# First q and k loads in halves of four heads, with one more unread matmul and a reordered column step, in an attention + MLP kernel

## The chip, the cores and the metric

The kernel runs on one core of a Trainium2 chip. The metric is the device time of one launch in microseconds (us). Before the change it is 356.62 us, the median of three runs (356.17 to 357.84).

The engines of the core work side by side, each through its own list of instructions in order: PE (TensorE, matrix products; its weight loads are listed as PEld), DVE (VectorE), ACT (ScalarE), POOL (GpSimd) and SP (SyncE). POOL, SP and ACT also issue DMA transfers, which all run on the same 16 DMA engines.

## What is computed

Attention with a forgetting gate over 8 batches of 8 heads, 576 positions and head size 64, and then a two-layer MLP on all 4608 rows:

```python
scores = scale * np.matmul(q, k.transpose(0, 1, 3, 2))
cum = np.cumsum(np.log(np.clip(f, 0.0001, 1.0)), axis=-1)
decay = cum[:, :, :, None] - cum[:, :, None, :]
scores = np.where(causal, -1000000000.0, scores + decay)   # causal: above the diagonal
attn = softmax(scores)
x = (attn @ v), heads side by side                # 4608 x 512
h = x @ w_in                                      # 512 -> 2048
out = (h - np.tanh(h)) @ w_out                    # 2048 -> 512
```

Inputs and output are float32; the kernel computes in float16 with float32 sums.

## The kernel before

**Batches.** Batch 0 has code of its own, written so that work begins as soon as the first rows are there; the others go by pairs of heads (`slot`, L481), and the MLP's steps (`step`, L455: `mlp1`, then `mlp2`, for 512 rows at a time) are dealt out among them by hand. The order on every engine is the order in which the code is written out (L497 to L601); there is no scheduler.

**Loading batch 0.** Each block of 128 positions of q and of k (the fifth has 64) is one DMA issued by POOL through `load_first` (L88): 128 positions by 8 heads by 64 values, converted from float32 to float16 on the way. The order on POOL is: q and k of block 0; a select that makes the identity matrix `id16` (L129), needed by every transpose; q and k of block 1; a select that makes the triangle `tri16` (L133), the mask of the diagonal; q and k of block 2; then, mixed with blocks 3 and 4, the five blocks of v (`load_v`), the first half of w_in (`load_win`, L523), q and k of batch 1 (`load_qk`), the second half of w_in, later v and q, k of batch 1, w_out (L575), and at last q and k of batch 2 whole (`LOADS`, L200), which is issued in `slot`. A DMA uses one of eight semaphores in turn, so an issue waits until the eighth DMA before it has landed.

**Using it.** `half0(ib, a, ...)` (L269) takes block `ib` and half `a` of the heads: `trans0` (L247) turns four heads of q and four of k with eight PE transposes (L254) into one PSUM tile, and two copies, one for q and one for k (`copy0`, L260, on DVE or ACT), bring them to `QT` and `KT`. `scores0` (L274) multiplies them (L282), adds the mask on the diagonal with a second matmul (L285, `neg16` times `tri16`), and takes the exponential on ACT (L287). `values0` (L289) multiplies with v (L295).

**The decay columns.** The running sum of log f goes into extra columns of q and k, so that the score's matmul adds it. `decay_turn` (L171) turns it on PE (L176), and `decay_cols(b0, b1)` (L178) writes the columns for blocks b0 to b1 with three DVE operations (L181, L183, L184). Blocks 0 and 1 get theirs before the first transposes; blocks 2 to 4 at L508.

**Unread matmuls.** `spin(n)` (L221) issues n matmuls of 128 by 512 on a constant, whose result nobody reads. Eight stand at the start (L497) and one before the first transposes (L503).

**Batch 1 and 2.** Their q and k come in whole rows and are turned by `trans` (L227, six transposes each, L236): those of batch 2's first pair of heads stand in the fourth slot of batch 1, between score and MLP matmuls.

Of the kernel before, what the change touches and what calls it, by code (L numbers as in the profile page):

```python
# [22 lines left out]
def kernel(  # L23
# [10 lines left out]
    nc = tc.nc  # L34
    P = 128

    B, H, S, D = q.shape
# [28 lines left out]
    ps_m = ctx.enter_context(tc.tile_pool(name="ps_m", bufs=3, space=PSUM))  # L66
# [4 lines left out]
    XR = wpl.tile([P, NCH, RING], FP16)  # L71

    HH = H // 2
    raw = [[qkp.tile([P, RW], FP16, tag=f"{x}n{i}", name=f"{x}n{i}") for i in range(2)] for x in "qk"]
    qn, kn = ([t[0:S // NT6, :].rearrange("p (h n d) -> p h n d", h=H, n=NT6) for t in ts] for ts in raw)
    qa, ka = (t[0][:, 0:NJ * H * AW].rearrange("p (n h d) -> p n h d", n=NJ, h=H) for t in raw)
# [8 lines left out]
        pn = min(P, S - n * P)  # L85
        nc.gpsimd.dma_start(out=dst[0:pn, n, h0:h1, 0:D], in_=src[b, h0:h1, n * P:n * P + pn, :].rearrange("h p d -> p h d"))  # L86

    def load_first(dst, src, n):  # L88
        p0 = max(0, (n + 1) * P - S)
        nc.gpsimd.dma_start(out=dst[p0:P, n, :, 0:D],  # L90
                            in_=src[0, :, n * P:(n + 1) * P - p0, :].rearrange("h p d -> p h d"))

    def turn_block(dst, src, b, n):
        pn = min(P, S - n * P)
# [5 lines left out]
    def load_v(b, n):  # L100
        load_block(vn[b % 2], v, b, n)
# [22 lines left out]
    nc.vector.memset(ones16, 1.0)  # L124
    nc.vector.memset(id16, 0.0)
    nc.vector.memset(tri16, 0.0)
    load_first(qa, q, 0)
    load_first(ka, k, 0)
    nc.gpsimd.affine_select(out=id16, in_=id16, compare_op=ALU.not_equal,  # L129
                            fill=1.0, base=0, pattern=[[-1, P]], channel_multiplier=1)  # L130
    load_first(qa, q, 1)
    load_first(ka, k, 1)
    nc.gpsimd.affine_select(out=tri16, in_=tri16, compare_op=ALU.is_ge,  # L133
                            fill=BIG, base=0, pattern=[[1, P]], channel_multiplier=-1)
    nc.vector.memset(vn[0][:, :, :, D:VW], 1.0)
# [35 lines left out]
    def decay_turn(blocks):  # L171
        if not CT:
            CT.append(ps_tr.tile([P, UW], FP32, tag="tr", name="ct"))
        for ib in blocks:
            t0 = min(ib * P, S - P)
            nc.tensor.transpose(out=CT[0][:, ib * H:(ib + 1) * H], in_=cum[0:H, t0:t0 + P], identity=id32)  # L176

    def decay_cols(b0, b1):  # L178
        ct = CT[0][:, b0 * H:b1 * H].rearrange("p (n h) -> p n h", h=H)
        hi = ka[:, b0:b1, :, D]  # L180
        nc.vector.tensor_scalar(out=qa[:, b0:b1, :, D + 2], in0=ct, scalar1=inv_qscale,  # L181
                                scalar2=-SHIFT * inv_qscale, op0=ALU.mult, op1=ALU.add)
        nc.vector.tensor_scalar_mul(out=hi, in0=ct, scalar1=inv_qscale)  # L183
        nc.vector.scalar_tensor_tensor(out=ka[:, b0:b1, :, D + 1], in0=ct, scalar=inv_qscale, in1=hi,  # L184
                                       op0=ALU.mult, op1=ALU.subtract)
# [16 lines left out]
    for b in range(2, B):  # L202
        p0 = (b - 1) * NPAIR
# [17 lines left out]
    def spin(n):  # L221
        av = ps_av.tile([P, 2, 512], FP32, tag="av", name="spin")
        for _ in range(n):
            nc.tensor.matmul(out=av[:, 0, :].rearrange("p (a n) -> p a n", n=P), lhsT=one128[:, 0, :],  # L224
                             rhs=one128.to_broadcast([P, UW // P, P]))
# [21 lines left out]
    def trans0(ib, a, pool, engs):  # L247
        p0 = max(0, (ib + 1) * P - S)
        pn = P - p0
        t32 = pool.tile([P, UW], FP32, tag="tr" if pool is ps_tr else "m", name="t32")  # L250
        t16 = t32.bitcast(FP16)[0:D + 3, 0:H * pn].rearrange("p (x h n) -> p x h n", x=2, h=HH)
        for x, src in enumerate((qa, ka)):
            for h in range(HH):
                nc.tensor.transpose(out=t16[:, x, h, :], in_=src[p0:P, ib, a * HH + h, 0:D + 3],  # L254
                                    identity=id16[p0:P, p0:P])
        T0[(ib, a)] = t16, engs
# [3 lines left out]
    def copy0(ib, a, x):  # L260
        w = min(P, S - ib * P)
        t16, engs = T0[(ib, a)]
        to = (QT, KT)[x][0][:, a * HH:(a + 1) * HH, ib * P:ib * P + w]
        if engs[x] == "A":
            nc.scalar.activation(out=to, in_=t16[:, x, :, :], func=AF.Copy)
        else:
            nc.vector.tensor_copy(out=to, in_=t16[:, x, :, :])

    def half0(ib, a, pool, engs):  # L269
        trans0(ib, a, pool, engs)  # L270
        copy0(ib, a, 0)
        copy0(ib, a, 1)

    def scores0(ib, ti):  # L274
        w = min(P, S - ib * P)
        n = UW // w
        ps = ps_sc.tile([P, 512], FP32, tag="sc", name="ps")
        e = aex.tile([P, 512], FP16, tag="e", name="e")
        todo = [(h, j) for h in range(H) for j in range(ib + 1)][n * ti:n * ti + n]
        for i, (h, j) in enumerate(todo):  # L280
            at = slice(i * w, (i + 1) * w)
            nc.tensor.matmul(out=ps[:, at], lhsT=KT[0][:, h, j * P:(j + 1) * P],  # L282
                             rhs=QT[0][:, h, ib * P:ib * P + w], start=True, stop=(j < ib))
            if j == ib:
                nc.tensor.matmul(out=ps[:, at], lhsT=neg16, rhs=tri16[:, 0:w], start=False, stop=True)  # L285
            E[(0, h, j, ib)] = e[:, at]
        nc.scalar.activation(out=e, in_=ps, func=AF.Exp, scale=qscale)  # L287

    def values0(ib):  # L289
        w = min(P, S - ib * P)  # L290
        av = ps_av.tile([P, 2, 512], FP32, tag="av", name="av")
        av = av[0:w, :, 0:HH * (D + 1)].rearrange("p i (h d) -> p i h d", h=HH)
        for h in range(H):
            for j in range(ib + 1):
                nc.tensor.matmul(out=av[:, h // HH, h % HH, :], lhsT=E.pop((0, h, j, ib)),  # L295
                                 rhs=vn[0][:, j, h, 0:D + 1], start=(j == 0), stop=(j == ib))
# [205 lines left out]
    nc.vector.tensor_scalar_mul(out=neg16, in0=id16, scalar1=-BIG)  # L502
    spin(1)  # L503
    half0(0, 0, ps_m, "VA")
    half0(0, 1, ps_m, "VV")
    scores0(0, 0)
    decay_turn((2, 3, 4))
    decay_cols(2, NJ)  # L508
    half0(1, 0, ps_m, "VV")
    scores0(0, 1)  # L510
    half0(1, 1, ps_m, "VV")
    load_first(qa, q, 2)
    load_first(ka, k, 2)
    load_v(0, 0)
    load_v(0, 1)
    load_first(qa, q, 3)
    load_first(ka, k, 3)
    load_v(0, 2)
    load_v(0, 3)
    load_first(qa, q, 4)  # L520
    load_first(ka, k, 4)
    load_v(0, 4)
    load_win(0, DFF // 2)  # L523
    for h in (0, 2):
# [105 lines left out]
```

## Time and profile before

| | |
|---|---|
| median of three runs | 356.62 us |
| the profiled execution | 356.36 us |
| its span, first to last instruction | 354.6 us |
| PE busy | 347.9 us (98%) |
| ACT busy | 222.9 us (63%) |
| DVE busy | 192.6 us (54%) |
| POOL busy | 150.3 us (42%) |
| moved by DMA | 38.70 MB in 148,583 packets |
| chain that ended last | PE 92%, DVE 4%, ACT 3% |

The profile is of one execution. A timeline row gives start and duration in us, the engine, the line, the operation, what it writes and reads, and how often; in brackets the engine's idle time before it and what ended it. `x2` means that two instructions are merged in the row. A matmul's duration runs to its end in the pipeline, so that neighbours overlap: what a row costs PE is the distance to the next start. Of a DMA issued by POOL the row's duration is POOL's work to issue it; the landing is given apart, counted from the issue's start. In rows of shares over 40 slices each digit is the busy share in tenths, 9 for 90% and more.

### The profile page before, as it was taken

Reading aid. Unit: us, or ns where it says so; the run is one execution under the profiler, and the core shown is the slowest. Engines: PE = TensorE matmul, PEld = TensorE weight load, DVE = VectorE, ACT = ScalarE, POOL = GpSimd, SP = SyncE. Lnnn points to the kernel's source line nnn. Section 1 sums busy time; section 2 is a strip of 40 time slices with the busy share of each in tenths; the row PEclk is TensorE's granted clock in tenths of the full one; section 3 lists DMA queues with packets and bytes.
Section 4 is the critical chain, followed back from the end, with each engine's and each line's share of the span. In section 5 each row is a group of like instructions: output and inputs, shape, how many; then the busy total and the mean of one; then the engine's idle time right before and its main releaser. Section 6 shows DMA issues by size and latency. Waiting matters only on the chain.

```text
span 354.6 us, 7878 instructions
## 1 busy us (share of the span) xinstructions
PE 347.9 (98%) x3002; PEld 203.1 (57%) x3002; DVE 192.6 (54%) x364; ACT 222.9 (63%) x411; POOL 150.3 (42%) x291
## 2 busy tenths in 40 slices
PE   7989999999999999999999999999999999999996
PEld 4978886555555555555558865555555554444443
DVE  6587887449851676167715681478137513812720
ACT  4587886357755885588557865786568734613620
POOL 8954523653477537662776277632222210000000
PEclk9999999999999999999999999999999999999999
DMA  9999999999299949998999979991220022011002
GB/s 91 143 202 187 205 183 153 158 179 151 28 108 173 149 87 114 146 151 114 76 152 183 115 59 140 167 142 31 88 74 16 8 74 76 2 53 66 2 30 89
DMA packets 148583, 38.70 MB, mean 109 GB/s; under 512 B 137346, under 2 KB 143042, under 8 KB 148546
## 3 DMA queue, kind: packets, MB, share of 16 engines
q0 software_dynamic: 100128, 18.36, 72.5%
q1 hardware_dynamic: 48338, 19.78, 29.0%
q8 instruction: 23, 0.38, 0.5%
q14 instruction: 14, 0.11, 0.2%
q10 hardware_dynamic: 80, 0.07, 0.1%
HBM read 36.85 MB, written 9.44 MB: 131 GB/s over the span
## 4 chain that ended last, share of the span: by engine, by line
PE 92%; DVE 4%; ACT 3%; issue 1%; ACTq 0%; DVEq 0%
PE ops L442 34%; PE hps L415 30%; PE ps L340 10%; PE av L368 7%; PE hps L401 3%; PE ps L282 1%; PE t L254 1%; ACT e L287 1%; DVE gt L391 1%; DVE KT L245 1%; PE spin L224 1%; PE ops L426 1%; PE t L236 1%; ACT th L389 1%; PE av L295 1%; PE ps L285 1%
## 5 line engine op out<-in xcount | busy, mean ns | idle before, releaser
L442 PE MATMUL ops<-wout,gt 128*128 128x512 f16 x560 | 136.8, 378 | 0.0
L391 DVE TENSOR_TENSOR gt<-hps,th 128x512 f16<-128x512 f32 x144 | 99.0, 690 | 58.9 <-ACT th L389 58.2
L349 ACT ACTIVATE e<-ps 128x512 f16<-128x512 f32 x168 | 99.3, 594 | 46.9 <-PE ps L340 40.1
L415 PE MATMUL hps<-XR,win 128*128 128x512 f16 (+1 forms) x576 | 125.6, 355 | 0.2
L389 ACT ACTIVATE th<-hps 128x512 f32<-128x512 f32 x144 | 86.0, 597 | 29.0 <-PE hps L415 22.9
L359 POOL TENSOR_SCALAR_AFFINE_SELECT e<-e 128x128 f16<-128x128 f16 x144 | 48.7, 338 | 102.7 <-ACT e L349 100.2
L442 PEld LDWEIGHTS <-gt 128*128 128x128 f16 x560 | 50.3, 97 | 51.0
L415 PEld LDWEIGHTS <-win 128*128 128x128 f16 x576 | 52.3, 97 | 44.3 <-issue 0.5
L340 PE MATMUL ps<-QT,KT 67*128 67x512 f16 (+1 forms) x336 | 70.7, 277 | 0.4 <-ACT e L349 0.2
L340 PEld LDWEIGHTS <-KT 67*128 67x128 f16 x336 | 32.8, 98 | 33.5 <-DVE KT L245 0.2
L446 ACT ACTIVATE ost<-ops 128x512 f32<-128x512 f32 x35 | 20.9, 597 | 36.4 <-PE ops L442 36.4
L374 DVE TENSOR_SCALAR rs<-av 128x10 f32<-128x10 f32 x28 | 4.6, 164 | 68.4 <-PE av L368 68.3
L86 POOL DMA_DIRECT2D vn<-in_v_dram x40 | 34.2, 862 | 11.4 <-DMA win<-in_moe_w_in_dram 3.6
L368 PEld LDWEIGHTS <-e 128*128 128x128 f16 x784 | 28.1, 97 | 5.5
L368 PE MATMUL av<-vn,e 128*128 128x65 f16 x784 | 29.1, 193 | 0.0
L86 POOL DMA_DIRECT2D qn<-in_q_dram x25 | 21.2, 848 | 11.3 <-PE t L236 6.1
L376 DVE TENSOR_TENSOR xn<-av,rs 128x640 f16<-128x640 f32 x28 | 23.1, 825 | 1.0
L86 POOL DMA_DIRECT2D kn<-in_k_dram x25 | 21.3, 852 | 1.4 <-issue 1.2
L287 ACT ACTIVATE e<-ps 128x512 f16<-128x512 f32 x25 | 14.4, 596 | 6.6 <-PE ps L285 4.6
L401 PE MATMUL hps<-XR,win 128*128 128x256 f16 x128 | 16.6, 272 | 0.0
L282 PE MATMUL ps<-QT,KT 67*128 67x128 f16 (+1 forms) x120 | 12.0, 220 | 1.5 <-ACT e L287 0.7
L245 DVE COPY QT<-t 64x576 f16<-64x576 f16 x12 | 9.6, 801 | 6.5 <-PE t L236 5.1
(83 smaller groups left out, 221.3 us busy)
## 6 DMA issues: line engine op xcount, KB each, us to landing
out_dram<-ost SPq DMA_DIRECT2D x35, 256.0 KB
vn<-in_v_dram POOLq DMA_DIRECT2D x32, 128.0 KB, 5.5
qn<-in_q_dram POOLq DMA_DIRECT2D x24, 128.0 KB, 3.8
kn<-in_k_dram POOLq DMA_DIRECT2D x24, 128.0 KB, 4.8
win<-in_moe_w_in_dram POOLq DMA_DIRECT2D x2, 1024.0 KB, 12.2
wout<-in_moe_w_out_dram POOLq DMA_DIRECT2D x4, 512.0 KB, 11.9
XR<-xn SPq DMA_TRANSPOSE x56
qn<-in_q_dram POOLq DMA_DIRECT2D x1, 576.0 KB, 17.6
```

What stands on the lines that cost most here:

```text
L86: nc.gpsimd.dma_start(out=dst[0:pn, n, h0:h1, 0:D], in_=src[b, h0:h1, n * P:n * P + pn, :].rearrange("h p d -> p h d"))
L340: nc.tensor.matmul(out=ps[:, col:col + n], lhsT=KT[b % 2][0:D + 3, h, j * P:(j + 1) * P], rhs=QT[b % 2][0:D + 3, h, i0:i0 + n], start=True ...
L349: nc.scalar.activation(out=e[:, lo:hi], in_=ps[:, lo:hi], func=AF.Exp, scale=qscale)
L359: nc.gpsimd.affine_select(out=view, in_=view, compare_op=ALU.is_ge, fill=0.0, base=0, pattern=pat, channel_multiplier=-1)
L368: nc.tensor.matmul(out=av[:, a, ib, :], lhsT=E.pop((b, 2 * c + a, j, ib)), rhs=vn[b % 2][:, j, 2 * c + a, 0:D + 1], start=(j == 0), stop=( ...
L376: nc.vector.tensor_tensor(out=xn.rearrange("p i (a d) -> p a i d", a=2), in0=av[:, :, :, 0:D], in1=rs.to_broadcast([P, 2, NJ, D]), op=ALU. ...
L389: nc.scalar.activation(out=th, in_=hps, func=AF.Tanh, scale=-1.0)
L391: nc.vector.tensor_tensor(out=gt, in0=hps, in1=th, op=ALU.add)
L401: nc.tensor.matmul(out=hps[:, w * SB:(w + 1) * SB], lhsT=win[:, ci, ft * P:(ft + 1) * P], rhs=XR[:, ci, t * SB:(t + 1) * SB], start=(ci == ...
L415: nc.tensor.matmul(out=hps[:, o:o + n], lhsT=win[:, ci, s * P:(s + 1) * P], rhs=XR[:, ci, t:t + n], start=(ci == 0), stop=(ci == NCH - 1))
L442: nc.tensor.matmul(out=ops, lhsT=GT[(u, ft, m)], rhs=wout[:, ft, :], start=(ft == 0), stop=(ft == NFT - 1))
L446: nc.scalar.activation(out=ost, in_=ops, func=AF.Copy)
```

## The change

q and k of blocks 0, 1 and 2 of batch 0 are loaded in two DMAs of four heads each, where they were one of eight; blocks 3 and 4 stay whole. On POOL, the identity's select comes after the first half of block 0, and the triangle's select after both halves of block 1. One more unread matmul stands between the two halves of block 0 on PE. The columns of blocks 2 to 4 are written after the copies of block 1's first half instead of before them; the turn on PE that feeds them stays where it was.

```diff
+    HALVES = ((0, HH), (HH, H))
...
-    def load_first(dst, src, n):
+    def load_first(n, heads=((0, H),)):
         p0 = max(0, (n + 1) * P - S)
-        nc.gpsimd.dma_start(out=dst[p0:P, n, :, 0:D],
-                            in_=src[0, :, n * P:(n + 1) * P - p0, :].rearrange("h p d -> p h d"))
+        for h0, h1 in heads:
+            for dst, src in ((qa, q), (ka, k)):
+                nc.gpsimd.dma_start(out=dst[p0:P, n, h0:h1, 0:D],
+                                    in_=src[0, h0:h1, n * P:(n + 1) * P - p0, :].rearrange("h p d -> p h d"))
...
-    load_first(qa, q, 0)
-    load_first(ka, k, 0)
+    load_first(0, HALVES[0:1])
     nc.gpsimd.affine_select(out=id16, in_=id16, compare_op=ALU.not_equal,
                             fill=1.0, base=0, pattern=[[-1, P]], channel_multiplier=1)
-    load_first(qa, q, 1)
-    load_first(ka, k, 1)
+    load_first(0, HALVES[1:2])
+    load_first(1, HALVES)
     nc.gpsimd.affine_select(out=tri16, in_=tri16, compare_op=ALU.is_ge,
                             fill=BIG, base=0, pattern=[[1, P]], channel_multiplier=-1)
...
     half0(0, 0, ps_m, "VA")
+    spin(1)
     half0(0, 1, ps_m, "VV")
     scores0(0, 0)
     decay_turn((2, 3, 4))
+    half0(1, 0, ps_m, "VV")
     decay_cols(2, NJ)
-    half0(1, 0, ps_m, "VV")
     scores0(0, 1)
     half0(1, 1, ps_m, "VV")
-    load_first(qa, q, 2)
-    load_first(ka, k, 2)
+    load_first(2, HALVES)
     load_v(0, 0)
     load_v(0, 1)
-    load_first(qa, q, 3)
-    load_first(ka, k, 3)
+    load_first(3)
     load_v(0, 2)
     load_v(0, 3)
-    load_first(qa, q, 4)
-    load_first(ka, k, 4)
+    load_first(4)
```

## The prediction

> **What bounds the kernel now.** I read the page first (PE busy 98% of the 354.6 us span, the chain 92% PE), then the waits after 30 us (one wait over 0.15 us on PE), so nearly all idle time of PE lies in the first 30 us, the stage that the change touches. There I read PE's timeline.
>
> ```profile
> 6.62 0.61 PE L254 MATMUL t<-id,kn 128*67 128x128 f16 x4 [0.56 <-DVE neg L502]
> 8.37 0.29 PE L282 MATMUL ps<-QT,KT 67*128 67x128 f16 x1 [0.29 <-ACT KT L265]
> 10.61 0.31 PE L282 MATMUL ps<-QT,KT 67*128 67x128 f16 x1
> 10.71 0.31 PE L285 MATMUL ps<-tri,neg 128*128 128x128 f16 x1
> 13.98 0.22 PE L285 MATMUL ps<-tri,neg 128*128 128x128 f16 x1
> 14.04 0.28 PE L282 MATMUL ps<-QT,KT 67*128 67x128 f16 x2
> ```
>
> Each starts with start and duration in us. PE has two holes, before 6.62 and before 8.37. Matmuls of 128 columns start 0.11 us apart at 10.6 and 0.06 apart at 14: the clock doubles at about 13.2. (The granted clock is given as 1.00 in every window; the spacing says otherwise.)
>
> Then POOL, which issues every load of q, k, v and the weights, in order.
>
> ```profile
> 1.33 1.01 POOL L90 DMA_DIRECT2D qn<-in_q_dram  x1 [0.82 <-POOLq L614]
> ...
> 5.63 0.89 POOL L90 DMA_DIRECT2D qn<-in_q_dram  x1
> 6.51 0.88 POOL L90 DMA_DIRECT2D kn<-in_k_dram  x1
> 7.38 1.77 POOL L86 DMA_DIRECT2D vn<-in_v_dram  x2
> ...
> 13.24 0.77 POOL L90 DMA_DIRECT2D kn<-in_k_dram  x1
> 13.91 0.77 POOL L86 DMA_DIRECT2D vn<-in_v_dram  x1
> 14.58 0.86 POOL L188 DMA_DIRECT2D win<-in_moe_w_in_dram  x1
> 15.33 0.75 POOL L196 DMA_DIRECT2D qn<-in_q_dram  x1
> ```
>
> From 1.33 to 20 POOL does nothing but issue, two short selects aside. A whole block of 128 rows and 8 heads takes 0.87 us from start to start (5.63, 6.51, 7.38); the fifth block, 64 rows and half as many pieces, takes 0.67 (13.24, 13.91, 14.58). Half the pieces save a quarter.
>
> Last I asked where these loads come due. The whole of batch 2's q and k is issued at 37.23 and 38.01; the views of these two issues, q then k:
>
> ```profile
> who waited for it (us, times):
>   PEld L236: 0.2, 1
> ...
> DMA to landing us min/median/max: 17.6/17.6/17.6
> ```
> ```profile
> DMA to landing us min/median/max: 19.8/19.8/19.8
> ```
> ```profile
> 54.76 0.22 PE L343 MATMUL ps<-tri,neg 128*128 128x128 f16 x1
> 54.89 0.43 PE L236 MATMUL t<-id,qn 96*128 96x96 f16 x6
> ...
> 57.64 0.19 PE L343 MATMUL ps<-tri,neg 128*128 128x64 f16 x1
> 57.81 0.43 PE L236 MATMUL t<-id,kn 96*128 96x96 f16 x6
> ```
> ```profile
> DMA  9999999999999999999999999999999999999999
> ```
>
> 37.23 + 17.6 = 54.8 and 38.01 + 19.8 = 57.8: PE's transposes of them (L236) start at 54.89 and 57.81, the moment they land, with gaps of 0.13 and 0.17 us where the same mask matmul is followed 0.06 and 0.03 later elsewhere. So PE and the loads arrive together: the loads have no slack. The last row is the DMA engines' share in 40 slices of 16 to 58 us: never under 90%. From 16 us on this is one unbroken stream; whatever starts it later lands those two later.
>
> **The change, part by part.**
>
> *Halves on POOL.* Six loads become twelve. A half is [128 rows, 4 heads], 512 pieces; no row shows it. Bounds: half of a whole one, 0.44 (shift 0), and as much as a whole one, 0.87 (shift 5.2 us). The nearest rows are the fifth block (512 pieces, 0.67) and the 128x4 shape of wout, 0.74 us each when issued alone, win 0.75 (14.58 to 15.33). I take 0.72: 12 x 0.72 - 6 x 0.87 = 8.6 - 5.2 = 3.4 us. POOL's issues also wait for the eighth one before them to land (4.15 us idle before wout's at 32.66, ended by win's landing); eight halves take 5.8 us to issue and about 3.1 to land, so that wait isn't met. SP's queue has nothing moved. Everything behind it on POOL moves by the 3.4: v0 from 7.38 to 10.8, block 3's k from 9.97 to 13.4, the first weights from 14.58 to 18.0. With 0.67 it is 2.8. The triangle's select, which stood behind four loads (5.38), now stands behind eight: 1.33 + 0.86 + 0.74, the identity's select 0.4, then 6 x 0.72 end at 7.7, so the triangle is there at 8.0; its reader, the first mask matmul, ran at 8.45.
>
> The Trainium skill's page "DMA: Bandwidth & Descriptors" speaks on both sides. Its section on the anatomy of a software-issued DMA puts dispatch at some 50 ns and calls descriptor generation small, so by it six more issues are an estimated 0.3 us and the sum stays at 356.4. The rows above have 0.7 to 0.9 us of POOL for each issue and decide against that. Its rules for kernel authors say of two halves that they share the same engines and aren't worth splitting, which is the sum taken here.
>
> *The stream behind it.* Part of the 3.4 us is given back, because the DMA engines were somewhat behind in the first 17 us: block 3's k landed 4.5 us after its issue and the fifth v block, a half-size one, 4.3, where the first q had taken 3.6. A half-size load without a backlog is 3.6 - 0.2 (shorter issue) - 0.43 (half of the 0.87 between landings) = 3.0, so the backlog at the weights was 1.3 to 1.4 us. With slower issue it doesn't build. 3.4 - 1.4 = 2.0 us later for win and all that follows. Bounds: 0.8 (issue at 0.62, the smallest issue's spacing, 15.33 to 15.96: shift 2.2, less 1.4) and 3.4 (no backlog given back).
>
> *Who meets it.* win: 14.58 + 9.8 = 24.4, plus 2.0 is 26.4; first reader L401 at 27.34: hidden, 0.9 to spare. Batch 1's loads have 2.6 us and more (its last q 27.12 + 10.9 = 38.1 for 40.72): hidden; with 3.4 late it would cost 0.8. Batch 2's q and k have none: PE waits 2.0 us at 54.89. Behind that wait stands all of PE's order, and PE is 98% busy from there to the end, so it is paid in full.
>
> *The start.* The first halves land earlier: k's is issued at 2.2 and lands about 3.2 later, 5.4, where the whole landed at 2.34 + 4.1 = 6.5. Its transposes can follow q's at 5.86 instead of 6.62. The unread matmul costs one step of the spin, 3.60/8 = 0.43 (still at the slow clock), and fills the time to the second half of q (3.3 + 3.1 = 6.4): net at most 0.3. The first scores come 0.4 to 0.6 earlier. With the holes gone, the clock may double one step earlier; at 0.11 against 0.06 that is at most half of some 3.4 us, 1.7. But block 3's k lands at 13.4 + 3.7 to 4.1 = 17.1 to 17.5, and its transposes ran at 16.95: most of the lead is used up there, and what is left ends in the wait at 54.89. If nothing waited there the start would be worth 2.1 us.
>
> The Trainium skill's "TensorE: Matmul & The Clock Gate", Part 1, has a free-running window of 3.4 us, a busy one opening the clock: by it the opening moves from 13.2 to 9.8. Its Part 4 says that transposes don't count as busy; here half of the time from 9.8 to 13.2 was transposes (L254) and the clock opened all the same, so the trace doesn't bear that out.
>
> *Later columns moved.* DVE's three L181 to L184 operations, 0.67 us, go behind the copies of block 1's first half. Their reader is block 2's transposes (13.42 in this run): covered, 0.67 if not.
>
> **Sum.** 356.36 (the profiled execution, 354.6 of span and 1.8 around it) + 2.0 at the stream + 0 for the start = **358.4**. The profiled execution lies 0.26 under the median of the runs, 356.62. What a measurement can tell from no change here is about 0.5%, 1.8 us: the forecast stands on that border, at +1.8 against the median.
>
> **Rivals.**
> - *The stream catches up.* Issue costs under 0.65, or the engines' backlog was larger: late by 0 to 1.2, 356.4 to 357.6. For: some engines land over 1 us behind the others. Against: the nearest rows.
> - *Faster: the start's lead gets through.* If the loads of batch 2 don't come later but with the work, PE keeps 1.7 + 0.4 and ends at 354.3. It decides at 54.89: q would have to land by 52.8. For: the two holes and the late clock are real. Against: nothing issues batch 2's loads earlier, and a stream that has no free slice can't land 2 us sooner.
> - *Slower still.* Nothing of the backlog comes back: +3.4, 359.8; win (27.8) then also stops PE at 27.34.
> - *The halves land no sooner than wholes* (latency, not size): the start gains nothing, the stream is as late: 358.4.
>
> **Chances.** Forecast 0.58 (its own range 357.2 to 359.2, 0.36 of it over 358.4), catching up 0.17, faster 0.10 (0.08 beyond 0.5%), slower still 0.12, no sooner 0.03. So faster 0.08, within 0.5% 0.43, slower 0.49. The range goes from 356.0, which leaves out the faster case, to 359.6, which leaves out half of the slower one.
>
> **What would show it.** POOL: the starts of the halves 0.72 apart, v0's issue near 10.8, win's near 18. The landing of batch 2's q near 56.8 and L236 on it starting right then, after a wait of about 2 us. PE's spacing of 0.06 from about 10 instead of 13.2, and the lead gone by block 3. Wrong if win is issued before 16.8, if batch 2's q lands by 55, or if PE doesn't wait there.

## The result and the profile after

The changed kernel is slower: 360.81 us, the median of four runs (359.77 to 360.92), against 356.52 us before (356.17 to 357.84, four runs). The recorded ratio is 1.0107, 95% interval 1.0075 to 1.0139. One execution among the runs below, 452.3 us long at a mean granted clock of 0.753, was a slow one and is left out. The profiled execution took 360.92 us, span 359.2; that of before took 356.36, span 354.6. So 4.56 us have to be found between these two.

From the page of the changed kernel, PE's busy time and the chain that ended last, by engine and by line:

```profile
PE 347.8 (97%) x3003; PEld 202.2 (56%) x3003; DVE 193.0 (54%) x364; ACT 223.0 (62%) x411; POOL 154.4 (43%) x297
...
PE 80%; DMA 12%; POOL 5%; DVE 1%; issue 1%; ACT 1%; POOLq 0%; DVEq 0%; ACTq 0%
```

PE's work is the same (347.8 us, 347.9 before); what grew is time in which it waits. The chain was 92% PE before. Now it runs through DMA (12%) and POOL (5%): it goes back from a waiting PE to a landing, and from the landing to POOL's list of issues. POOL's timeline of the changed kernel (start, duration, engine, line, operation):

```profile
4.21 0.76 POOL L93 DMA_DIRECT2D kn<-in_k_dram  x1
4.94 0.77 POOL L93 DMA_DIRECT2D qn<-in_q_dram  x1
...
7.88 0.36 POOL L135 TENSOR_SCALAR_AFFINE_SELECT tri<-tri 128x128 f16<-128x128 f16 x1
...
11.07 1.84 POOL L87 DMA_DIRECT2D vn<-in_v_dram  x2
...
13.68 0.98 POOL L93 DMA_DIRECT2D kn<-in_k_dram  x1
...
18.29 0.92 POOL L190 DMA_DIRECT2D win<-in_moe_w_in_dram  x1
...
42.04 0.79 POOL L198 DMA_DIRECT2D qn<-in_q_dram  x1 [1.69 <-PE ps L342]
42.82 0.77 POOL L198 DMA_DIRECT2D kn<-in_k_dram  x1
```

A half of four heads costs POOL 0.73 us from start to start (4.21, 4.94). The first v is issued 3.7 us later than before (11.07 for 7.38), block 3's k also (13.68 for 9.97), and w_in (18.29 for 14.58). Batch 2's q and k are 4.8 us later (42.04 for 37.23).

PE's timeline of the changed kernel, the rows where it waits, the first w_in matmul (L403), and batch 2's transposes (L238); in brackets the idle time before a row and what ended it:

```profile
8.29 0.22 PE L287 MATMUL ps<-tri,neg 128*128 128x128 f16 x1 [0.59 <-POOL tri L135]
...
12.36 0.38 PE L256 MATMUL t<-id,kn 128*67 128x128 f16 x4 [0.68 <-DMA kn<-in_k_dram]
...
13.86 0.41 PE L256 MATMUL t<-id,kn 128*67 128x128 f16 x4 [0.51 <-DMA kn<-in_k_dram]
...
16.29 0.22 PE L284 MATMUL ps<-QT,KT 67*128 67x128 f16 x1 [0.40 <-ACT e L289]
...
17.52 0.41 PE L256 MATMUL t<-id,qn 128*67 128x128 f16 x4 [0.73 <-DMA qn<-in_q_dram]
18.36 0.44 PE L256 MATMUL t<-id,kn 128*67 128x128 f16 x4 [0.42 <-DMA kn<-in_k_dram]
...
30.36 0.71 PE L403 MATMUL hps<-XR,win 128*128 128x256 f16 x5
...
59.14 0.43 PE L238 MATMUL t<-id,qn 96*128 96x96 f16 x6 [1.15 <-DMA qn<-in_q_dram]
...
62.70 0.43 PE L238 MATMUL t<-id,kn 96*128 96x96 f16 x6 [0.61 <-DMA kn<-in_k_dram]
```

Before, no wait of PE behind 8.37 was over 0.24 us. Two of its rows, block 3's transposes of k and the first w_in matmul:

```profile
16.95 0.39 PE L254 MATMUL t<-id,kn 128*67 128x128 f16 x4
...
27.34 0.71 PE L401 MATMUL hps<-XR,win 128*128 128x256 f16 x5
```

In the changed kernel blocks 2 and 3, the blocks behind the new issues, stop it again and again. A table by stretches of the same kernel (length, busy time of each engine, then the granted clock, DMA share, GB/s) shows what the holes bring with them:

```profile
12.00:18.60 6.60, 3.88 (x56) 3.16 (x57) 2.57 (x7) 3.01 (x6) 6.60 (x10) 1.00 1.99 127
18.60:22.00 3.40, 3.40 (x44) 3.40 (x42) 2.32 (x7) 0.89 (x2) 3.40 (x6) 0.50 1.61 135
```

PE is busy for 3.88 of 6.60 us, and then the clock falls to half for 3.4 us, in which PE works without a stop and gets 1.7 us worth of full-speed work done. The account: block 3's transposes of k at 18.36, where they were at 16.95 (+1.4); half clock, +1.7 at most; the first w_in matmul at 30.36 where it was at 27.34 (+3.0). Then the two waits at batch 2's q and k, 1.15 and 0.61: +4.8, less the 0.3 of small gaps that stood there before, makes 4.5 of the 4.56.

The landing of batch 2's loads, from the view of their issuing line:

```profile
DMA to landing us min/median/max: 17.1/18.4/19.8
```

42.04 + 17.1 = 59.1 and 42.82 + 19.8 = 62.6, against 54.8 and 57.8 before: 4.3 and 4.8 us later, and PE starts on each as it lands.

### The profile page after: what moved, and what is told of

The parts are those of the page before. It is cut to its first block, busy times and chain, and to the rows that moved or that the text cites. A ratio compares the mean times of both kernels' runs of the same rounds, so it can differ in the third digit from the quotient of the medians.

```text
span 359.2 us, 7888 instructions
## 1 busy us (share of the span) xinstructions
PE 347.8 (97%) x3003; PEld 202.2 (56%) x3003; DVE 193.0 (54%) x364; ACT 223.0 (62%) x411; POOL 154.4 (43%) x297
## 3 DMA queue, kind: packets, MB, share of 16 engines
q0 software_dynamic: 100224, 18.36, 68.9%
## 4 chain that ended last, share of the span: by engine, by line
PE 80%; DMA 12%; POOL 5%; DVE 1%; issue 1%; ACT 1%; POOLq 0%; DVEq 0%; ACTq 0%
PE ops L444 33%; PE hps L417 30%; PE ps L342 9%; PE av L370 6%; DMA kn<-in_k_dram 6%; DMA vn<-in_v_dram 4%; DMA win<-in_moe_w_in_dram 3%; POOL qn L93 2%; POOL kn L93 2%; POOL vn L87 1%; PE ops L428 1%; DVE gt L393 1%; PE t L238 0%; DVE KT L247 0%; ACT th L391 0%
## 5 line engine op out<-in xcount | busy, mean ns | idle before, releaser
L289 ACT ACTIVATE e<-ps 128x512 f16<-128x512 f32 x25 | 14.3, 595 | 10.6 <-PE ps L287 5.3
L403 PE MATMUL hps<-XR,win 128*128 128x256 f16 x128 | 16.6, 272 | 0.0
L247 DVE COPY KT<-t 64x576 f16<-64x576 f16 x15 | 12.0, 799 | 2.6 <-PE t L238 2.5
```

The lines of the kernel that those rows point to most:

```text
L247: nc.vector.tensor_copy(out=to, in_=of)
```

## The experiments

In the expectations of the first four, S is the theory that six more issues on POOL move every later load; C, that an early opened clock closes again; T, that the DMA engines pay for small transfers. All times are medians; ratios, with their 95% interval, are those recorded against runs of the kernel before on the same chip, and need not be the quotient of two medians.

### One part alone: the unread matmul and the later columns

```diff
     half0(0, 0, ps_m, "VA")
+    spin(1)
...
-    decay_cols(2, NJ)
     half0(1, 0, ps_m, "VV")
+    decay_cols(2, NJ)
```

> The kernel before with the unread matmul between block 0's halves and the later columns, all loads whole. Theory S (six more issues on POOL move every later load by 3.7 us; PE meets them at block 3 and at batch 2's q and k): no shift on POOL, win issued at 14.6, so 356.0 to 356.7. Theory C (the fuller start opens the clock early, later holes close it again for 3.4 us, which costs some 1.7): 357.5 to 358.5, with a stretch of doubled matmul spacing after 15 us. Theory T (the DMA engines pay more for smaller transfers): as S, 356.0 to 356.7.

357.31 us (ratio 1.000, 0.9965 to 1.0035): no difference that can be measured, with a median between the expectations of S and of C. In the profiled execution the first w_in matmul ran at 24.97, 2.4 us earlier than in the kernel before. PE's row at batch 2's q:

```profile
56.19 0.39 PE L236 MATMUL t<-id,qn 96*128 96x96 f16 x5 [3.03 <-DMA qn<-in_q_dram]
```

The whole lead became a wait of 3.03 us, and the clock stood at 0.50 from 57.5 to 60.9 behind it: this execution, at 358.93, is the slowest of the ten. Whatever PE wins at the start ends here, as the prediction had said of its start; over all executions these two parts show neither cost nor gain as the loads stand.

### The halves alone

The change without the unread matmul and with the columns in their old place.

> All three blocks in halves, the selects where the change puts them, but no added unread matmul and the columns in their old place. S: win issued near 18.3, batch 2's q lands near 59, 360.3 to 361.0, as the change. C: 358.5 to 359.5, some 1.7 less than the change. T: as S.

359.90 us (1.0076, 1.0048 to 1.0105), 0.4 below the range of S and 0.4 above that of C. The halves carry most of the loss: by the medians 3.4 us, where the change costs 4.3, and the two intervals overlap. PE waits 1.70 and 1.19 us at batch 2's q and k.

### Only block 0 in halves

```diff
-    load_first(1, HALVES)
+    load_first(1)
...
-    load_first(2, HALVES)
+    load_first(2)
```

> The change with block 0 alone in halves, blocks 1 and 2 whole: two more issues instead of six. S: POOL later by a third of 3.7, 1.2 us, win issued near 15.8; 357.6 to 358.1. C: as the change less nothing, 360 to 361, if the clock opens and closes as there; T: a third of 4.3, 357.7 to 358.1.

358.21 us (1.0032, 1.0010 to 1.0054), with w_in issued at 15.85: just above the ranges of S and T, and far below that of C. PE's rows at block 3's k and batch 2's q:

```profile
17.27 0.41 PE L256 MATMUL t<-id,kn 128*67 128x128 f16 x4 [1.60 <-DMA kn<-in_k_dram]
...
57.23 0.43 PE L238 MATMUL t<-id,qn 96*128 96x96 f16 x6 [1.91 <-DMA qn<-in_q_dram]
```

Two more issues move the stream by 1.3 us and cost 1.7 by the medians, 1.1 by the ratio; six move it by 3.7 and cost 4.3 by the medians, 3.8 by the ratio. The loss goes with the shift, at about one for one.

### POOL kept busy, all loads whole

```diff
+    idle = cst.tile([P, 192], FP16)
+    for _ in range(9):
+        nc.gpsimd.memset(idle, 0.0)
...
     load_first(ka, k, 2)
+    for _ in range(5):
+        nc.gpsimd.memset(idle, 0.0)
     load_v(0, 0)
```

The nine stand behind the triangle's select, the five ahead of the first v; together they hold POOL for 4.4 us.

> The kernel before, all loads whole, with fourteen memsets of a tile that nobody reads on POOL (0.27 us each by the rows of el: nine ahead of block 2's q, five ahead of the first v, 3.8 us in all). No transfer is smaller or more. S: POOL's issues behind them 3.8 us later, win near 18.3, 360.3 to 361.2. C: 356.5 to 357. T: 356.0 to 357.0, POOL's time being hidden.

361.25 us (1.0115, 1.0077 to 1.0153). Not one transfer is smaller, and the loss is as large as the change's: T falls, and so does C as the whole cause (both had expected 357 us at most). S had expected 360.3 to 361.2 for 3.8 us of POOL's time. What POOL's time does to what is queued behind it is enough. The Trainium skill's page "DMA: Bandwidth & Descriptors" (Anatomy of one DMA) calls dispatch and generation of a software-issued DMA small beside its latency. The runs don't contradict that the landing takes longer than the issue (2.9 to 3.5 us against 0.73 for a half of k), but in a list of some twenty issues it is the issue, 0.73 us for a half, that adds up. PE's rows of this kernel:

```profile
18.99 0.41 PE L258 MATMUL t<-id,qn 128*67 128x128 f16 x4 [1.88 <-DMA qn<-in_q_dram]
...
59.28 0.42 PE L240 MATMUL t<-id,qn 96*128 96x96 f16 x6
```

Here the whole loss is made in front: PE waits for block 3, the first w_in matmul comes at 31.81 (27.34 before), and at batch 2's q there is no wait left. So there are two places, and the next runs part them.

### Batch 2's loads taken off the end of the stream

The same edit in four kernels: batch 2's q and k are issued after the first of the four w_out loads, where they stood behind the last.

```diff
-    LOADS = {(NPAIR, 5): [lambda: load_qk(qn, q, 2, 0, H)],
-             (NPAIR, 6): [lambda: load_qk(kn, k, 2, 0, H)]}
+    LOADS = {}
...
     for t in range(0, NFT, 4):
+        if t == 4:
+            load_qk(qn, q, 2, 0, H)
+            load_qk(kn, k, 2, 0, H)
         load_wout(t, t + 4)
```

To the kernel with whole loads, the unread matmul and the later columns:

> The kernel with whole loads, the extra unread matmul and the later columns, and batch 2's q and k issued after the first of the four w_out loads in place of long behind the last. Theory S (what the halves cost is the time at which later loads land, and the start's lead was lost only in the wait of 3.03 us for batch 2's q): q lands before 50 us, no wait over 0.3 us on it, the lead of 2.4 us goes through: 354.1 us (353.4 to 355.0), first w_in matmul near 25.0. Rival W (another load takes over as the bound: the last three w_out groups now land up to 8 us later, or the next v): a new wait of 1 us or more on wout or vn between 55 and 65 us, and 355.8 to 357. Rival N (batch 2's load wasn't the limit): 357.3 as without the move.

To the changed kernel:

> The changed kernel with batch 2's q and k issued after the first w_out load. Theory S splits the loss of 4.4 us in two: 3.0 us by the first w_in matmul (late blocks 2 and 3 and the clock shut again) and 1.2 + 0.6 us of waits at batch 2's q and k. The move takes only the second: 359.0 us (358.6 to 359.7), the first w_in matmul still near 30.4. Rival W (the w_out groups or the next v become the wait): 360 to 361. Rival B (all of the loss is batch 2's wait, the start catches up): 356.4 to 357.

To the kernel before:

> The kernel before with batch 2's q and k issued after the first w_out load: the move alone. The kernel before has no wait over 0.15 us there, so theory S gives 356.3 us (355.9 to 356.7), no difference that can be measured. If the move is worth 1 us or more by itself, the waits of 0.13 and 0.17 us understate what the load held up. Rival W: slower, 357 to 358.

To the change with only block 0 in halves:

> The change with only block 0 in halves, and batch 2's q and k issued after the first w_out load. Without the move it ran 358.2 us with waits of 1.91 and 0.65 us for batch 2's q and k. Theory S: both go, 355.7 us (355.2 to 356.4), and it stays behind the kernel with whole loads and the move by the 1.60 us that block 2's k stops PE at 17.3 us. Rival W: 357 to 358.5.

Measured: 354.90 us (0.9949, 0.9923 to 0.9975), 359.95 (1.0117, 1.0054 to 1.0179), 355.42 (0.9966, 0.9938 to 0.9994) and 356.10 (0.9978, 0.9944 to 1.0013). In the four profiles no wait at batch 2's q or k is left, and w_out lands in time (its last group at 58.6 to 60.4 us).

The first expectation was 354.1, and half of its ten runs stand there (353.9 to 354.2), four at 355.6 to 356.1, one, the profiled one, at 357.6. In that one PE waited 2.09 us for block 3's k at 16.86, and this stretch shows the clock:

```profile
16.50:20.00 3.50, 3.14 (x38) 3.14 (x39) 1.67 (x5) 0.60 (x1) 2.83 (x5) 0.51 1.16 170
```

The third was a miss: the move alone was expected to bring nothing and brought 1.2 us. The profile of it suggests why. PE's rows at the first scores:

```profile
7.98 0.23 PE L281 MATMUL ps<-QT,KT 67*128 67x128 f16 x1 [0.69 <-ACT KT L264]
8.04 0.22 PE L284 MATMUL ps<-tri,neg 128*128 128x128 f16 x1
8.10 0.22 PE L281 MATMUL ps<-QT,KT 67*128 67x128 f16 x1
```

Matmuls start 0.06 apart at 8.0: the clock is open, in a kernel whose instructions up to here are those of the kernel before, which had 0.11 at 10.6 in its profile. The clock opened early in this execution and late in that one. As far as these profiles show, with batch 2's loads at the end of the stream an early clock ends in a wait there (the first experiment); with these loads out of the way it comes through. The fastest execution here takes 353.9 us, as does the fastest of the first of these kernels; the unread matmul and the later columns add nothing to the move that can be told.

The second run decides the main point. The changed kernel without the wait at batch 2 still takes 359.95 us, 4.5 more than the kernel before with the same edit. (Four executions: 359.1, 359.8, 360.1 and 363.3.) Its PE row at the first v, and its stretches:

```profile
16.55 0.60 PE L296 MATMUL av<-vn,e 128*128 128x65 f16 x8 [2.63 <-DMA vn<-in_v_dram]
```
```profile
15.00:21.80 6.80, 5.10 (x56) 4.94 (x56) 2.17 (x7) 2.32 (x4) 6.45 (x10) 0.50 1.94 138
21.80:28.00 6.20, 5.59 (x104) 4.81 (x102) 5.84 (x21) 4.62 (x8) 4.23 (x8) 1.00 1.17 201
```

The late loads of batch 0 hold PE back: a hole of 2.63 us at the first v, and 6.8 us at half clock. Not all of the hole is the late issue: this v landed 5.6 us after it, in the changed kernel's profile 3.8. Nothing of the stream stops it, since w_in lands at 27.3 and PE comes to it at 30.9. Theory S had split the loss, 3.0 in front and 1.8 at batch 2; the edit took 0.9 by the medians, which the two intervals (1.0075 to 1.0139 and 1.0054 to 1.0179) can't tell from nothing.

### The stream alone late

The 14 memsets now stand behind the last v of batch 0 and ahead of w_in, so that q, k and v of batch 0 are issued as before.

```diff
+    idle = cst.tile([P, 192], FP16)
+    for _ in range(14):
+        nc.gpsimd.memset(idle, 0.0)
     load_win(0, DFF // 2)
```

> The kernel before with 14 unread memsets on POOL (about 3.8 us) behind the last v of batch 0 and ahead of w_in: all of q, k and v of batch 0 is issued as before, and only the stream behind it is late. Theory P (the prediction's term: 1.4 us of such a shift is given back by the DMA engines, the rest is paid at batch 2's q): q of batch 2 lands near 57.2 and 358.8 us (358.2 to 359.3). Theory F (nothing is given back): q lands near 58.6 and 360.2 us (359.6 to 360.9). Theory D (the loss of the change is made before 30 us by the late blocks of batch 0; the stream behind makes the shift good or has room): at most 357.6 us.

360.56 us (1.0114, 1.0081 to 1.0148). POOL's and PE's rows:

```profile
14.56 4.47 POOL L525 MEMSET idle<- 128x192 f16 x14
19.02 0.77 POOL L188 DMA_DIRECT2D win<-in_moe_w_in_dram  x1
```
```profile
28.09 0.83 PE L401 MATMUL hps<-XR,win 128*128 128x256 f16 x6 [0.43 <-DMA win<-in_moe_w_in_dram]
...
42.31 0.26 PE L236 MATMUL t<-id,qn 96*128 96x96 f16 x2 [0.68 <-DMA qn<-in_q_dram]
...
58.59 0.30 PE L236 MATMUL t<-id,qn 96*128 96x96 f16 x3 [2.01 <-DMA qn<-in_q_dram]
...
62.19 0.30 PE L236 MATMUL t<-id,kn 96*128 96x96 f16 x3 [0.66 <-DMA kn<-in_k_dram]
```

The stream started 4.4 us late (19.02 for 14.58), batch 2's q landed 3.7 late (58.53 for 54.84) and its k 4.4 late, and the four waits add up to 3.78 us. Of the 1.4 us that the prediction had coming back, 0.7 came back at q and nothing at k. Theory F holds, P and D fall.

Then the same kernel with batch 2's loads issued early:

> The run before last but with batch 2's q and k issued after the first w_out load: batch 0's q, k and v are issued as in the kernel before, the stream behind them is 4.4 us late (w_in issued at 19.0), and batch 2's loads no longer stand at its end. Of its loss, 3.8 us were waits: 0.43 on w_in, 0.68 on batch 1's q, 2.01 and 0.66 on batch 2's q and k. If the late stream is paid at batch 2's loads, the last two go: 356.5 us to 357.9 (the kernel before with the early issue has 355.4; plus 1.1 to 2.5, the upper end for a clock that opens early and then waits longer for w_in), and what the changed kernel with the early issue has beyond that, 359.95, is the start's own share. If the late stream costs its 4 us at another place too: 359 us or more.

357.91 us (1.0044, 1.0031 to 1.0058), the upper end of the first case. What is left is the wait for w_in, longer in an execution with an early clock:

```profile
28.05 0.39 PE L400 MATMUL hps<-XR,win 128*128 128x256 f16 x2 [1.51 <-DMA win<-in_moe_w_in_dram]
```

The runs side by side:

| what is late | batch 2's loads last | issued early |
|---|---|---|
| nothing (the kernel before) | 356.5 | 355.4 |
| nothing, with the unread matmul and later columns | 357.3 | 354.9 |
| block 0 in halves: batch 0 and the stream by 1.3 us | 358.2 | 356.1 |
| the stream alone, by 4.4 us | 360.6 | 357.9 |
| the change: batch 0 and the stream by 3.7 us | 360.8 | 360.0 |

(The kernel before stood at 356.4 to 356.8 in the sets of runs, so differences between rows are uncertain by some tenths.) With batch 2's loads issued early, a late stream costs 2.5 us (355.4 to 357.9), and a late batch 0 with it 4.5 (355.4 to 360.0). Each place is enough for about the whole loss: the stream by its own run, at 360.6, batch 0 by two traces in which nothing of the stream makes PE wait (POOL kept busy from the start, and the changed kernel with early loads). The change makes both late, and they don't add, since a PE that is late in front waits less at batch 2.

### Filling the holes

Two unread matmuls ahead of each of five waiting places (both halves of blocks 2 and 3, and the first v), in the changed kernel with batch 2's loads early:

```diff
+    spin(2)
     half0(2, 0, ps_m, "VV")
...
+    spin(2)
     half0(2, 1, ps_tr, "VV")
```

> The changed kernel with batch 2's q and k issued after the first w_out load, and two more unread matmuls of 512 columns (about 0.2 us each at the fast clock) before each of the five places where PE waits for blocks 2 and 3 and for v. Without them it ran 359.95 us, with the clock at half speed from 15.0 to 21.8. If the shut clock carries 1.7 us of the loss or more: 357.2 to 358.4, clock open through. If the loss is the late landing alone (block 3's k at 18.3 to 18.8, v behind it): 359.5 to 361, with the clock open all the same.

359.33 us (1.0074, 1.0048 to 1.0101), between the two expectations. In the profiled execution, of 360.0 us, PE still waited 1.89 us for the first v and the clock shut:

```profile
18.00:21.50 3.50, 3.50 (x26) 2.55 (x24) 0.75 (x2) 1.27 (x3) 3.38 (x6) 0.52 1.90 139
```

The mean granted clock recorded for each execution tells how often that happened: 1.7 us lost in a span of 358 take 0.005 from it, and the profiled one has 0.995. Five executions at 0.999 to 1.000 took 357.7 to 358.9 us, three at 0.995 took 359.7 to 360.0, two at 0.991 took 361.4 and 361.9. So the fill left the clock open in half of them, and each shutting cost 1.5 us or a little more. With none, the middle one of the five, 358.4, is still 3.0 above the 355.4 of the kernel before with early loads. The larger part of the front's loss is then the late landings, as far as the fill itself, whose price wasn't measured here, is cheap.

Four unread matmuls ahead of block 3 in the fastest kernel so far:

```diff
+    spin(4)
     half0(3, 0, ps_m, "VV")
```

> Whole loads, the extra unread matmul, the later columns, batch 2's q and k issued early, and four unread matmuls before block 3's first transposes. Without these four its ten runs stood at 353.9 to 354.2 (five), 355.6 to 356.1 (four) and 357.6 (one), and in the last the clock shut for 3.41 us after a wait of 2.1 us for block 3's k; half of 3.41 is 1.7, the distance of the groups. If these groups are executions with none, one and two such shuttings, the fill leaves the first group alone: 354.2 us (353.9 to 354.9). If they are not, the median stays at 354.9 or rises by the 0.8 us of the four matmuls to 355.7.

354.85 us (0.9945, 0.9923 to 0.9968), which fits both expectations. Seven of the eight executions stand between 354.65 and 355.32; the eighth is the one of 452.3 us and the only one profiled, so no row of this kernel is read. The groups at 355.6 and 357.6 are gone, at a price of 0.7 us in the fastest: the median is that without the fill. That the groups were one and two shuttings of the clock doesn't hold: without the fill, the execution at 357.62 has a mean clock of 0.995 and in its profile one shutting and a wait of 2.09 us, and the four at 355.6 to 356.1 have 1.00, as the fastest have. What slowed these four isn't shown; a clock that opens late doesn't lower this mean (before's profile opens at 13.2 and reads 1.00). This kernel and the one without the fill both beat the kernel before, with whole loads; their difference can't be told.

## Why the prediction was wrong in its size

The forecast was slower at 358.4 us, by late loads that PE meets at batch 2's q. The direction held, and so did the mechanism, late loads that PE meets at batch 2's q; the time lies 1.2 us above the range's end. What PE lost ahead of that place, 3.0 us, the prediction had at 0.

- **Halves on POOL, 0.72 each, shift 3.4.** 0.73 to 0.77 each, shift 3.7. Right in kind, 0.3 short. The rule on halves that the prediction quotes from the Trainium skill ("DMA: Bandwidth & Descriptors", Rules for kernel authors) is written for halves of the partitions, and here the halves are of the heads; no run here tests it, and the sum doesn't use it.
- **1.4 us of the shift given back.** This is the step that failed. The prediction reasoned that with slower issue the DMA engines' backlog doesn't build. The halves of k did land sooner after their issue (2.9 to 3.5 us), but the whole loads behind them built it again: block 3's k took 4.6 us from issue to landing, 4.5 before. w_in's first half landed 3.1 us late (27.5 for 24.4), so at most 0.6 had come back there; its second half took 14.6 us to land as before, and nothing had. By batch 2 the lateness had grown to 4.3 and 4.8, for which the prediction had no term: the issue of batch 2's q waits for the eighth DMA before it, a v of batch 1, which landed at 41.5 for 36.6, 12.8 us after its issue where it had taken 11.0. The run with the stream alone late measured the term without the halves: 0.7 at q, 0 at k. With this term at 0 and the shift of 3.7, the prediction's own sum is 356.36 + 3.7 = 360.1; with the lateness measured at batch 2 it is 356.36 + 4.3 to 4.8 = 360.7 to 361.2. The profiled execution took 360.92.
- **PE waits 2.0 at batch 2's q.** The place was right, the wait 1.15 at q and 0.61 at k, because PE came 3.0 us late itself.
- **The start, 0 in sum.** It lost 3.0 us by the first w_in matmul. The first half of k landed at 5.1 (5.4 forecast), and the triangle came at 8.24 (8.0 forecast), where its reader waited 0.59. But block 3's k landed at 18.3, not 17.1 to 17.5: issued 0.3 later than forecast, and 4.6 us on the way for 3.7 to 4.1, the same backlog term. The prediction compared that landing with PE's place of before and stopped there; it had no term for the holes at blocks 2 and 3 shutting the clock again. It didn't lengthen the sum, since the stream's lateness covers it, but in the kernel with early loads the start is the whole loss. (3.60/8 is 0.45, not 0.43; nothing hangs on it. And half of the 3.4 us ahead of the clock's opening being transposes doesn't show that transposes count: the other half was mostly score matmuls.)
- **w_in and batch 1's loads hidden; the columns covered.** All held in the changed kernel, w_in and batch 1's loads because PE was late too: with only the stream late they stopped it for 0.43 and 0.68 us.
- **The rivals.** *Slower still* had the mechanism, nothing of the backlog coming back, and was 1.0 short at 359.8 since the shift grew; w_in, which it had stopping PE too, didn't. *Faster* was ruled out because nothing issues batch 2's loads earlier: when they are issued earlier, whole loads with the unread matmul take 354.9. *The stream catches up* and *halves land no sooner* fell. For the price of an issue the prediction went by the rows' 0.7 to 0.9 us, and 0.73 for a half bears that out.

## What to carry to other kernels

Where one engine issues a long list of loads, splitting the first of them moves all the others; count the issues on that list and carry the shift undiminished to the first load without slack (here it even grew, from 3.7 to 4.3 and 4.8 us). Look for every place where loads and work arrive together, not only the last: here the late blocks and the late stream were each worth the whole loss, so repairing one alone brought at most 0.9 us of 4.3 back. A lead won at the start is worth nothing until the load that meets it later is issued earlier: the two edits together brought 0.5%, the earlier issue alone 0.3%, which the intervals don't tell apart, and the edit at the start alone none that could be measured.

## What the runs showed of the hardware

- **The clock's opening is a matter of the execution.** The same instructions ran at 0.11 us spacing at 10.6 us in one profile and at 0.06 at 8.0 in another. So one profile, here that of before with its late clock, can leave out a wait that other executions have.
- **Short holes can shut it.** In the changed kernel the clock fell to half at 18.6 with no wait over 0.73 us in the 10 us before. The Trainium skill's page "TensorE: Matmul & The Clock Gate" (Why this matters for your kernels) asks for no idle gaps over about 3 us to keep the clock up. This trace doesn't agree: waits of 0.40, 0.73 and 0.42 us, 1.55 of the last 3.4, were enough. They don't always shut it: the kernel with block 0 in halves waited 1.60 and 1.91 us, and its clock stayed at 1.00 throughout.
- **Landings scatter.** Block 3's k, issued at 9.9 us, landed at 14.4 in one execution and at 16.8 in another with the same issues ahead of it, and the second stopped PE for 2.09 us.
